# Token sums ahead of the output scale, a second token buffer and a later widening of z on GpSimd and VectorE

## The chip, the cores and the metric

The kernel runs on one core of a Trainium2 chip. The metric is the device time of one execution in microseconds, and the median of the runs counts. A core has TensorE (matrix products), VectorE, ScalarE and GpSimd, each with its own in-order queue, and SyncE (SP), whose queue issues most transfers here. TensorE writes to PSUM, the other engines read it from there; GpSimd works on SBUF alone.

## What is computed

```python
def reference(q, k, v, w_in, w_out, w_in2, w_out2, g_ln):     # cut to what matters
    # windowed attention: 4 batches, 8 heads, 576 positions, head size 64 (plain and dilated masks)
    x = attention(q, k, v)                     # 2304 tokens x 512
    h = x @ w_in                               # 512 x 2048
    x = (h - np.tanh(h)) @ w_out               # 2048 x 512
    h = x @ w_in2                              # 512 x 1024: the second layer
    e = np.exp(h - h.max(-1, keepdims=True))
    solu = h * e / (e.sum(-1, keepdims=True) + 1e-09)
    mu = solu.mean(-1, keepdims=True)
    var = ((solu - mu) ** 2).mean(-1, keepdims=True)
    return ((solu - mu) / np.sqrt(var + 1e-06) * g_ln) @ w_out2    # 1024 x 512
```

## The kernel before

Attention and the first layer take the first 507 us; the result y goes to a buffer in device memory, and the weights of the second layer are prepared beside the end of the first. The change lies in the second layer, which runs over nine pairs of token tiles. A pair is 256 tokens, an odd tile (2i + 1) and an even tile (2i) of 128 each. All products are done in a split form, a high and a low part of each operand with three matmuls in place of one.

`load_y` (L512 to L517) loads a pair of y into `yr`, one buffer. `split_y` (L519 to L541) forms combinations of the pair's four quarter blocks, for a scheme in which seven products take the place of eight. Its part 0 has four GpSimd operations on 128x256 elements (L530: three sums or differences into `ysm`, one back into `yr`), a VectorE copy of a high part (L537) and a GpSimd difference for the low part (L538). Parts 2 and 1 are a copy and a difference each: part 2 reads what the fourth sum wrote into `yr`, part 1 reads `ysm` (128x768).

`mm3(i)` (L639 to L681) runs the seven products of pair i on TensorE, six matmuls each, in the order p1, p6, p5, p7, p4, p2, p3 of the code's bank names (p3 is added into p5's bank). Four PSUM banks take turns, so the fifth product waits until VectorE's `u2` (L655) has read its bank, and the sixth until `u3` (L663) has read its own. The tree sums (`neg_add`, L636) add banks to h with the sign turned and take the minimum along the way. Then come `softmax_e` (exponential on ScalarE, L686), `softmax_u` (product with e, VectorE, L691), `softmax_z` (mean taken off, L697, L698) and `square` (ScalarE, L707, with a sum).

`fac` (L709) turns that sum on GpSimd into the variance and, with a power, into the factor `sc`. `split_z` (L741) splits the scaled z into two fp16 parts `ab` (ScalarE L745, VectorE L746), which a DMA transposes (SP, L749); `put_z` (L751) widens the high part on ScalarE (L756) and the low part on VectorE (L757). `rest` (L715) computes the output's scale `g` from the sums on GpSimd, six or seven operations on one column. `mm4` (L759) is the output product, 48 matmuls a pair, with a scaled copy out of PSUM (L769) and the store (L770). The tiles of pairs 0 and 8 go another way: `trz` (L728) transposes z on TensorE, without the factor in it.

The order on each engine is that in which the code issues. The loop at L784, for pair i: `square` and both `fac` of pair i + 1, parts 1 and 2 of `split_y(i + 2)` where i < 2, both `split_z`, both `rest`, a load where i < 2, the output products of pair i, and `mm3(i + 2)`. Inside that `mm3`, from pair 3 on, stand `split_y` part 0 of the next pair behind the second product, parts 1 and 2 and the load behind `u2`; `put_z` of the odd tile stands behind the third product, `put_z` of the even tile behind the fifth.

Of the kernel before, what the change touches and what calls it, by code (L numbers as in the profile page):

```python
# [7 lines left out]
F32 = mybir.dt.float32  # L8
F32R = mybir.dt.float32r
I32 = mybir.dt.int32  # L10
F16 = mybir.dt.float16
# [29 lines left out]
def tile_kernel(ctx: ExitStack, tc: tile.TileContext, qk, vw, cst, w_in, w_out, w_in2, w_out2, g_ln, out):  # L41
# [471 lines left out]

    def load_y(j):
        if j < NP:
            y_raw[j] = p2.tile([128, KD, YT], F32, tag="yr", name=f"yr{j}", bufs=1)
            nc.sync.dma_start(out=y_raw[j], in_=y_dr[:, :, j * YT:(j + 1) * YT])  # L517

    def split_y(j, parts=range(3)):  # L519

        if j >= NP:
            return
        r = y_raw[j]
        if 0 in parts:
            y = yt[j] = p2.tile([128, 2, 7, 2, TT], F32R, tag="yt", name=f"yt{j}")
            sm = y_sm[j] = p2.tile([128, 3, 2, TT], F32, tag="ysm", name=f"ysm{j}", bufs=1)
            a11, a21, a22 = r[:, 0:2, 0:TT], r[:, 0:2, TT:YT], r[:, 2:4, TT:YT]
            for o, a, b, op in ((sm[:, 0], a21, a22, ALU.add), (sm[:, 1], sm[:, 0], a11, ALU.subtract),
                                (sm[:, 2], a11, a21, ALU.subtract), (a21, r[:, 2:4, 0:TT], sm[:, 1], ALU.subtract)):
                nc.gpsimd.tensor_tensor(out=o, in0=a, in1=b, op=op)  # L530
        y, sm = yt[j], y_sm[j]
        yh = y[:, 0].rearrange("p s k t -> p (s k) t")
        yl = y[:, 1].rearrange("p s k t -> p (s k) t")
        for p, sl, v in ((0, slice(0, 4), r[:, :, 0:TT]), (2, slice(4, 8), r[:, :, TT:YT]),
                         (1, slice(8, 14), sm.rearrange("p s k t -> p (s k) t"))):
            if p in parts:
                nc.vector.tensor_copy(out=yh[:, sl], in_=v)  # L537
                nc.gpsimd.tensor_tensor(out=yl[:, sl], in0=v, in1=yh[:, sl].bitcast(F32), op=ALU.subtract)  # L538
        if 2 in parts:
            y_raw.pop(j)  # L540
            y_sm.pop(j)  # L541


    p2 = None
    nxt = []
    moe = None
    slot = 0
# [62 lines left out]
    sb = ctx.enter_context(tc.tile_pool(name="sb", bufs=1, space=PSUM, side="left", reuse_waits="tile"))  # L610
    zo = ctx.enter_context(tc.tile_pool(name="zo", bufs=2, space=PSUM, side="left", reuse_waits="tile"))
    p3 = ctx.enter_context(tc.tile_pool(name="p3", bufs=2, side="left", reuse_waits="tile"))
    st = {}

    def prod(ps, y, blk, w, first=True):
# [23 lines left out]
    def mm3(i, mid=()):  # L639

        y = yt.pop(i)
        for t in range(2):
            st[2 * i + t] = {}
        mid = dict(mid)
        b0, b1 = bank(sa, "b0", i, "p1"), bank(sa, "b1", i, "p6")
        prod(b0, y, 0, "b11")
        prod(b1, y, 5, "t2")
        if i > 2:
            split_y(i + 1, (0,))
        u2 = p3.tile([128, 512], F32, tag="u2", name=f"u2_{i}", bufs=1)  # L650
        u3 = p3.tile([128, 512], F32, tag="u3", name=f"u3_{i}", bufs=1)
        b2, b3 = bank(sb, "b2", i, "p5"), bank(sb, "b3", i, "p7")
        c = p3.tile([128, 512], F32, tag="c", name=f"c_{i}", bufs=1)
        nc.scalar.copy(out=c, in_=b0)
        nc.vector.tensor_tensor(out=u2, in0=b1, in1=c, op=ALU.add)  # L655
        if i > 2:
            split_y(i + 1, (1, 2))
            load_y(i + 2)
        prod(b2, y, 4, "t1")
        if 0 in mid:  # L660
            mid[0]()
        prod(b3, y, 6, "t3")
        nc.vector.tensor_tensor(out=u3, in0=b3, in1=u2, op=ALU.add)  # L663
        neg_add(i, 1, 1, b2, u3)
        b1 = bank(sa, "b1", i, "p4")
        prod(b1, y, 3, "t4")
        neg_add(i, 1, 0, b1, u3)
        if 1 in mid:
            mid[1]()
        softmax_e(2 * i + 1)  # L670
        b3 = bank(sb, "b3", i, "p2")
        prod(b3, y, 1, "b21")
        neg_add(i, 0, 0, b3, c)
        softmax_u(2 * i + 1)
        prod(b2, y, 2, "b22", first=False)
        neg_add(i, 0, 1, b2, u2)
        softmax_e(2 * i)
        softmax_z(2 * i + 1)
        square(2 * i + 1)
        softmax_u(2 * i)  # L680
        softmax_z(2 * i)  # L681
# [30 lines left out]
        nc.gpsimd.tensor_scalar(out=var, in0=var, scalar1=1.0 / FF2, scalar2=1e-36, op0=ALU.mult, op1=ALU.max)  # L712
        nc.gpsimd.tensor_tensor(out=sc, in0=var, in1=half, op=ALU.pow)

    def rest(i):  # L715

        d = st[i]
        ssum, sc, var, g = (d["sml"][:, c:c + 1] for c in (1, 4, 5, 6))
        nc.gpsimd.tensor_scalar(out=ssum, in0=ssum, scalar1=1e-9, scalar2=1e-3, op0=ALU.add, op1=ALU.mult)
        nc.gpsimd.tensor_tensor(out=ssum, in0=ssum, in1=ssum, op=ALU.mult)  # L720
        nc.gpsimd.tensor_tensor(out=ssum, in0=ssum, in1=var, op=ALU.add)
        nc.gpsimd.tensor_tensor(out=ssum, in0=ssum, in1=half, op=ALU.pow)
        nc.gpsimd.tensor_tensor(out=var, in0=var, in1=sc, op=ALU.mult)
        nc.gpsimd.tensor_tensor(out=g, in0=ssum, in1=var, op=ALU.mult)
        if i // 2 in (0, NP - 1):
            nc.gpsimd.tensor_tensor(out=g, in0=g, in1=sc, op=ALU.mult)

    def trz(i):  # L728

# [11 lines left out]
    def split_z(i):  # L741

        d = st[i]
        ab = p3.tile([128, 2, FF2], F16, tag="ab", name=f"ab{i}")
        nc.scalar.activation(out=ab[:, 0], in_=d["hn"], func=AF.Copy, scale=d["f"])  # L745
        nc.vector.scalar_tensor_tensor(out=ab[:, 1], in0=d["hn"], scalar=d["f"], in1=ab[:, 0], op0=ALU.mult,  # L746
                                       op1=ALU.subtract)
        t = d["zt"] = p3.tile([128, 2 * NF2, TT], F16, tag="zt", name=f"zt{i}")
        nc.sync.dma_start_transpose(out=t, in_=ab.rearrange("p a n -> p (a n)"))  # L749

    def put_z(i):  # L751

        d = st[i]
        z = d["z"] = p3.tile([128, 2, NF2, TT], F32R, tag="z", name=f"z{i}")
        t = d["zt"].rearrange("p (a j) t -> p a j t", a=2)
        nc.scalar.copy(out=z[:, 0], in_=t[:, 0])  # L756
        nc.vector.tensor_copy(out=z[:, 1], in_=t[:, 1])  # L757

    def mm4(i):  # L759
        d = st.pop(i)  # L760
# [9 lines left out]
        nc.sync.dma_start(out=out[i * TT:(i + 1) * TT, :], in_=o)  # L770

    mm3(0)
    fac(1)

    def first():
        trz(1)
        square(0)
        fac(0)
        split_y(2, (0,))
        rest(1)  # L780
        rest(0)

    mm3(1, {0: first, 1: lambda: trz(0)})
    for i in range(NP):  # L784
        o, e = 2 * i + 3, 2 * i + 2
        if i + 1 < NP:
            square(e)
            fac(o)
            fac(e)
        if i < 2:  # L790
            split_y(i + 2, (1, 2))
        if i + 2 < NP:
            split_z(o)
            split_z(e)
        if i + 1 < NP:
            rest(o)
            rest(e)
        if i < 2:
            load_y(i + 3)
        mm4(2 * i + 1)  # L800
        if i + 2 == NP:
            trz(o)
        mm4(2 * i)
        if i + 2 == NP:
            trz(e)
        if i + 2 < NP:
            mm3(i + 2, {0: lambda: (put_z(o), i == 0 and split_y(3, (0,))), 1: lambda: put_z(e)})
    p2.release()
    sa.release()

# [74 lines left out]
```

## Time and profile before

| | |
|---|---|
| median of three runs | 733.3 us (730.84 to 733.91) |
| the profiled execution | 733.56 us, its span 731.8 us |
| TensorE busy, share of the span | 692.7 us, 95% |
| VectorE | 479.0 us, 65% |
| ScalarE | 383.9 us, 52% |
| GpSimd | 205.8 us, 28% |
| mean granted clock of TensorE | 0.985 |
| start of the second layer | 507.6 us |

The profile is of one execution. Names such as `u` or `sml` are those of the program's tiles, L663 is a line of the kernel, and a bracket gives the idle time ahead of an instruction and the operation whose end ended it. Busy shares are means over stages with different limits, so the second layer is read by itself. The granted clock is the share of TensorE's full speed that was granted in a stretch.

### The profile page before, as it was taken

The page shows a single profiled execution, that of the slowest core. Times are in us where ns is not written, and L with a number is a line of the kernel's source. Part 1 is how long each engine was busy: PE and PEld are TensorE (multiplying, and loading weights), DVE is VectorE, ACT ScalarE, POOL GpSimd, SP SyncE. Part 2 cuts the span into 40 slices and gives each one's busy share as a digit, 9 for nine tenths or more (in the row PEclk, how much of TensorE's full clock was granted, in tenths as well). Part 3 has the DMA queues.
Part 4 walks back from the last instruction along what each step waited for, and adds up shares of the span by engine and source line. Part 5 has one row for each costly group of instructions (what it writes and reads, how often), then busy time and mean ns, then how long its engine had stood idle before and what let it go on. Part 6 is the DMA issues. An engine that isn't in the chain of part 4 may idle for free.

```text
span 731.8 us, 11282 instructions
## 1 busy us (share of the span) xinstructions
PE 692.7 (95%) x3994; PEld 638.2 (87%) x3994; DVE 479.0 (65%) x1157; ACT 383.9 (52%) x917; POOL 205.8 (28%) x276
## 2 busy tenths in 40 slices
PE   6898999999999999999999999999988598889897
PEld 5688899999999999999999999999866487677786
DVE  5987676476666667766666435996857457655650
ACT  5778775465555555555555333764454254345441
POOL 2212311011110111111100103750385655576521
PEclk9999999999999999999999999999999899999999
DMA  9976521232223221322230025452031542443121
GB/s 278 340 247 201 173 73 54 64 110 65 66 65 108 66 59 44 105 66 65 66 108 2 1 71 173 147 171 73 1 68 50 139 74 56 104 115 87 24 77 43
DMA packets 59431, 71.36 MB, mean 98 GB/s; under 512 B 32112, under 2 KB 45936, under 8 KB 59376
## 3 DMA queue, kind: packets, MB, share of 16 engines
q1 hardware_dynamic: 56208, 65.93, 30.9%
q10 hardware_dynamic: 3168, 4.72, 1.8%
q8 instruction: 31, 0.51, 0.3%
q14 instruction: 24, 0.20, 0.1%
HBM read 53.86 MB, written 9.44 MB: 87 GB/s over the span
## 4 chain that ended last, share of the span: by engine, by line
PE 73%; DVE 9%; POOL 8%; issue 4%; ACT 3%; DMA 2%; SPq 0%; ACTq 0%; POOLq 0%; DVEq 0%
PE y L381 28%; PE h L354 26%; PE po L766 6%; PE sp L620 5%; PE pv L281 2%; PE tp L260 2%; PE qkp L225 2%; PE qkp L205 2%; POOL ysm L530 1%; DMA yr<-y_dr 1%; POOL yt L538 1%; DVE z L757 1%; DVE hn L636 1%; DVE p L210 1%; ACT e L686 1%
## 5 line engine op out<-in xcount | busy, mean ns | idle before, releaser
L354 PE MATMUL h<-x,wi 128*128 128x384 f32 x1152 | 222.8, 342 | 1.1 <-DVE t L365 1.1
L381 PE MATMUL y<-gs,wo 128*128 128x384 f32 x1152 | 218.7, 338 | 0.0
L354 PEld LDWEIGHTS h<-x,wi 128*128 128x128 f32 x1152 | 200.9, 190 | 2.4 <-DVE t L365 1.3
L381 PEld LDWEIGHTS y<-gs,wo 128*128 128x128 f32 x1152 | 201.1, 189 | 1.8
L253 POOL TENSOR_TENSOR p<-p,rs 96x512 f32<-96x512 f32 x47 | 57.3, 1219 | 353.7 <-DVE rs L251 331.8
L365 DVE TENSOR_TENSOR t<-h,t 128x384 f32<-128x384 f32 x96 | 53.0, 552 | 79.0 <-ACT t L362 78.9
L766 PE MATMUL po<-w2o_o,z 128*128 128x512 f32 x432 | 100.7, 392 | 0.0
L371 DVE TENSOR_TENSOR gs<-t,gs 128x384 fp32r<-128x384 f32 x96 | 82.2, 856 | 23.4 <-ACT gs L368 23.3
L766 PEld LDWEIGHTS po<-w2o_o,z 128*128 128x128 f32 x432 | 81.1, 188 | 17.7
L362 ACT ACTIVATE t<-h 128x384 f32<-128x384 f32 x96 | 47.0, 489 | 93.7 <-PE h L354 90.4
L245 ACT ACTIVATE p<-p,nm 96x128 f32<-96x128 f32 x192 | 75.2, 394 | 21.2 <-DVE nm L210 20.8
L368 ACT CAST gs<-t 128x384 fp32r<-128x384 f32 x96 | 49.2, 512 | 49.2 <-DVE t L365 49.0
L620 PE MATMUL sp<-w2i_b,yt 128*128 128x512 f32 x162 | 46.6, 440 | 17.3 <-DVE u L663 17.3
L620 PEld LDWEIGHTS sp<-w2i_b,yt 128*128 128x128 f32 x162 | 34.3, 216 | 27.7 <-DVE u L663 20.1
L620 PE MATMUL sp<-w2i_t,yt 128*128 128x512 f32 x216 | 52.6, 398 | 4.8 <-DVE u L655 4.0
L686 ACT ACTIVATE e<-hn,sml 128x1024 f32<-128x1024 f32 x18 | 20.8, 1155 | 68.2 <-DVE sml L636 47.9
L620 PEld LDWEIGHTS sp<-w2i_t,yt 128*128 128x128 f32 x216 | 41.1, 192 | 14.2 <-DVE u L655 4.4
L245 ACT ACTIVATION_READ_ACCUMULATOR p<-p,nm 96x1 f32 x192 | 36.5, 190 | 0.0
L205 PE MATMUL qkp<-qkr 64*96 64x128 f32 x160 | 29.4, 339 | 7.2 <-DMA qkr<-in_qk_dram 5.4
L205 PEld LDWEIGHTS qkp<-qkr 64*96 64x96 f32 x160 | 24.1, 205 | 11.7 <-DMA qkr<-in_qk_dram 5.8
L292 DVE TENSOR_TENSOR x<-pv,x 128x384 fp32r<-128x384 f32 x24 | 16.4, 703 | 25.7 <-ACT x L290 25.2
L746 DVE SCALAR_TENSOR_TENSOR ab<-hn,sml,ab 128x1024 f16<-128x1024 f32 x14 | 22.2, 1630 | 15.9 <-ACT ab L745 15.9
(89 smaller groups left out, 858.0 us busy)
## 6 DMA issues: line engine op xcount, KB each, us to landing
qkr<-in_qk_dram SPq DMA_DIRECT2D x28, 448.0 KB, 3.4
raw_wi<-in_w_in_dram SPq DMA_DIRECT2D x16, 511.8 KB, 7.0
raw_wo<-in_w_out_dram SPq DMA_DIRECT2D x16, 511.8 KB, 7.4
v<-in_vw_dram SPq DMA_DIRECT2D x48, 128.0 KB, 3.3
y_dr<-ys ACTq DMA_DIRECT2D x6, 768.0 KB, 3.9
yr<-y_dr SPq DMA_DIRECT2D x9, 512.0 KB, 4.9
out_dram<-o SPq DMA_DIRECT2D x18, 256.0 KB, 2.6
qkr<-in_qk_dram SPq DMA_DIRECT2D x20, 224.0 KB, 5.2
```

The lines of the kernel that those rows point to most:

```text
L205: nc.tensor.matmul(ps[:, b], d["r"][:64, b * NQ:(b + 1) * NQ], d["r"][:64, QC + b * NK:QC + (b + 1) * NK], start=True, stop=True)
L245: nc.scalar.activation(out=d["p"][:, b], in_=d["p"][:, b], func=AF.Exp, scale=-1.0, bias=d["nm"][:, b:b + 1], accum_out=d["sm"][:, b:b + 1])
L253: eng.tensor_tensor(out=d["p"], in0=d["p"], in1=d["rs"].unsqueeze(2).to_broadcast([NQ, 4, NK]), op=ALU.mult)
L354: nc.tensor.matmul(ps, w[:, a, k * 128:(k + 1) * 128], xt[g, k][:, b], start=(n == 0), stop=(n == 3 * KD - 1))
L362: nc.scalar.activation(out=t, in_=ps, func=AF.Tanh)
L365: nc.vector.tensor_tensor(out=t, in0=ps, in1=t, op=ALU.subtract)
L368: nc.scalar.copy(out=gs[:, 0], in_=t)
L371: nc.vector.tensor_tensor(out=gs[:, 1], in0=t, in1=gs[:, 0].bitcast(F32), op=ALU.subtract)
L381: nc.tensor.matmul(yb[g][m], wo[c][:, a, m * 128:(m + 1) * 128], gs[:, b], start=(c == 0 and i == 0), stop=(c == NF - 1 and i == 2))
L620: nc.tensor.matmul(ps, y[:, a, blk, kk], w2i[w, kk][:, b], start=first and q == 0, stop=q == 5, skip_group_check=not first)
L686: nc.scalar.activation(out=d["e"], in_=d["hn"], func=AF.Exp, bias=d["sml"][:, 0:1], scale=-1.0, accum_out=d["sml"][:, 1:2])
L766: nc.tensor.matmul(po, z[:, a, j], w2o[j][:, b], start=(q == 0), stop=(q == 3 * NF2 - 1))
```

## The change

In `first` and in the loop, part 0 of `split_y` is issued ahead of `rest`, and the `rest` of the even tile moves to the end of the next `mm3`, as the third of its middle steps. The yr of odd pairs from 3 on has a buffer of its own in pool `p3`, pair 3 is loaded when that pool is made, and the other loads come one pair earlier. `put_z` is cut in two: the high part of the odd tile behind the third product, its low part behind the fifth together with the high part of the even tile, and that one's low part behind the seventh. `fac` is left out for pairs 0 and 8, whose `rest` computes the scale in one power. `ab` uses the buffer of `e`.

```diff
--- before.py
+++ after.py
@@ -513,7 +513,8 @@
 
     def load_y(j):
         if j < NP:
-            y_raw[j] = p2.tile([128, KD, YT], F32, tag="yr", name=f"yr{j}", bufs=1)
+            pool = p3 if j > 2 and j % 2 else p2
+            y_raw[j] = pool.tile([128, KD, YT], F32, tag="yr", name=f"yr{j}", bufs=1)
             nc.sync.dma_start(out=y_raw[j], in_=y_dr[:, :, j * YT:(j + 1) * YT])
 
     def split_y(j, parts=range(3)):
@@ -541,7 +542,7 @@
             y_sm.pop(j)
 
 
-    p2 = None
+    p2 = p3 = None
     nxt = []
     moe = None
     slot = 0
@@ -610,6 +611,7 @@
     sb = ctx.enter_context(tc.tile_pool(name="sb", bufs=1, space=PSUM, side="left", reuse_waits="tile"))
     zo = ctx.enter_context(tc.tile_pool(name="zo", bufs=2, space=PSUM, side="left", reuse_waits="tile"))
     p3 = ctx.enter_context(tc.tile_pool(name="p3", bufs=2, side="left", reuse_waits="tile"))
+    load_y(3)
     st = {}
 
     def prod(ps, y, blk, w, first=True):
@@ -645,17 +647,15 @@
         b0, b1 = bank(sa, "b0", i, "p1"), bank(sa, "b1", i, "p6")
         prod(b0, y, 0, "b11")
         prod(b1, y, 5, "t2")
-        if i > 2:
-            split_y(i + 1, (0,))
         u2 = p3.tile([128, 512], F32, tag="u2", name=f"u2_{i}", bufs=1)
         u3 = p3.tile([128, 512], F32, tag="u3", name=f"u3_{i}", bufs=1)
         b2, b3 = bank(sb, "b2", i, "p5"), bank(sb, "b3", i, "p7")
         c = p3.tile([128, 512], F32, tag="c", name=f"c_{i}", bufs=1)
         nc.scalar.copy(out=c, in_=b0)
         nc.vector.tensor_tensor(out=u2, in0=b1, in1=c, op=ALU.add)
-        if i > 2:
+        if i > 1:
             split_y(i + 1, (1, 2))
-            load_y(i + 2)
+            load_y(i + 3)
         prod(b2, y, 4, "t1")
         if 0 in mid:
             mid[0]()
@@ -674,6 +674,8 @@
         softmax_u(2 * i + 1)
         prod(b2, y, 2, "b22", first=False)
         neg_add(i, 0, 1, b2, u2)
+        if 2 in mid:
+            mid[2]()
         softmax_e(2 * i)
         softmax_z(2 * i + 1)
         square(2 * i + 1)
@@ -712,18 +714,21 @@
         nc.gpsimd.tensor_scalar(out=var, in0=var, scalar1=1.0 / FF2, scalar2=1e-36, op0=ALU.mult, op1=ALU.max)
         nc.gpsimd.tensor_tensor(out=sc, in0=var, in1=half, op=ALU.pow)
 
-    def rest(i):
+    def rest(i, trz=False):
 
         d = st[i]
         ssum, sc, var, g = (d["sml"][:, c:c + 1] for c in (1, 4, 5, 6))
+        if trz:
+            nc.gpsimd.tensor_scalar(out=var, in0=var, scalar1=1.0 / FF2, scalar2=None, op0=ALU.mult)
         nc.gpsimd.tensor_scalar(out=ssum, in0=ssum, scalar1=1e-9, scalar2=1e-3, op0=ALU.add, op1=ALU.mult)
         nc.gpsimd.tensor_tensor(out=ssum, in0=ssum, in1=ssum, op=ALU.mult)
         nc.gpsimd.tensor_tensor(out=ssum, in0=ssum, in1=var, op=ALU.add)
-        nc.gpsimd.tensor_tensor(out=ssum, in0=ssum, in1=half, op=ALU.pow)
-        nc.gpsimd.tensor_tensor(out=var, in0=var, in1=sc, op=ALU.mult)
-        nc.gpsimd.tensor_tensor(out=g, in0=ssum, in1=var, op=ALU.mult)
-        if i // 2 in (0, NP - 1):
-            nc.gpsimd.tensor_tensor(out=g, in0=g, in1=sc, op=ALU.mult)
+        if trz:
+            nc.gpsimd.tensor_tensor(out=g, in0=ssum, in1=half, op=ALU.pow)
+        else:
+            nc.gpsimd.tensor_tensor(out=ssum, in0=ssum, in1=half, op=ALU.pow)
+            nc.gpsimd.tensor_tensor(out=var, in0=var, in1=sc, op=ALU.mult)
+            nc.gpsimd.tensor_tensor(out=g, in0=ssum, in1=var, op=ALU.mult)
 
     def trz(i):
 
@@ -741,20 +746,23 @@
     def split_z(i):
 
         d = st[i]
-        ab = p3.tile([128, 2, FF2], F16, tag="ab", name=f"ab{i}")
+        ab = d["e"].bitcast(F16).rearrange("p (a n) -> p a n", a=2)
         nc.scalar.activation(out=ab[:, 0], in_=d["hn"], func=AF.Copy, scale=d["f"])
         nc.vector.scalar_tensor_tensor(out=ab[:, 1], in0=d["hn"], scalar=d["f"], in1=ab[:, 0], op0=ALU.mult,
                                        op1=ALU.subtract)
         t = d["zt"] = p3.tile([128, 2 * NF2, TT], F16, tag="zt", name=f"zt{i}")
         nc.sync.dma_start_transpose(out=t, in_=ab.rearrange("p a n -> p (a n)"))
 
-    def put_z(i):
+    def put_z(i, part):
 
         d = st[i]
-        z = d["z"] = p3.tile([128, 2, NF2, TT], F32R, tag="z", name=f"z{i}")
+        if part == 0:
+            d["z"] = p3.tile([128, 2, NF2, TT], F32R, tag="z", name=f"z{i}")
         t = d["zt"].rearrange("p (a j) t -> p a j t", a=2)
-        nc.scalar.copy(out=z[:, 0], in_=t[:, 0])
-        nc.vector.tensor_copy(out=z[:, 1], in_=t[:, 1])
+        if part == 0:
+            nc.scalar.copy(out=d["z"][:, 0], in_=t[:, 0])
+        else:
+            nc.vector.tensor_copy(out=d["z"][:, 1], in_=t[:, 1])
 
     def mm4(i):
         d = st.pop(i)
@@ -770,41 +778,43 @@
         nc.sync.dma_start(out=out[i * TT:(i + 1) * TT, :], in_=o)
 
     mm3(0)
-    fac(1)
 
     def first():
         trz(1)
         square(0)
-        fac(0)
         split_y(2, (0,))
-        rest(1)
-        rest(0)
 
     mm3(1, {0: first, 1: lambda: trz(0)})
     for i in range(NP):
         o, e = 2 * i + 3, 2 * i + 2
+        last = i + 2 == NP
         if i + 1 < NP:
             square(e)
-            fac(o)
-            fac(e)
-        if i < 2:
-            split_y(i + 2, (1, 2))
-        if i + 2 < NP:
-            split_z(o)
-            split_z(e)
-        if i + 1 < NP:
-            rest(o)
-            rest(e)
-        if i < 2:
-            load_y(i + 3)
+            if last:
+                rest(o, True)
+                rest(e, True)
+            else:
+                fac(o)
+                if i == 0:
+                    split_y(2, (1, 2))
+                fac(e)
+                if i == 0:
+                    rest(1, True)
+                    rest(0, True)
+                split_z(o)
+                split_z(e)
+                split_y(i + 3, (0,))
+                rest(o)
+                if i == 0:
+                    load_y(4)
         mm4(2 * i + 1)
-        if i + 2 == NP:
+        if last:
             trz(o)
         mm4(2 * i)
-        if i + 2 == NP:
+        if last:
             trz(e)
         if i + 2 < NP:
-            mm3(i + 2, {0: lambda: (put_z(o), i == 0 and split_y(3, (0,))), 1: lambda: put_z(e)})
+            mm3(i + 2, {0: lambda: put_z(o, 0), 1: lambda: (put_z(o, 1), put_z(e, 0)), 2: lambda: (put_z(e, 1), rest(e))})
     p2.release()
     sa.release()
```

## Rows read from the trace of the kernel before

**Rows 1.** Waits of TensorE from 490 us: us in total, times, longest.
```profile
PE sp L620 <- DVE u L663: 17.3, 6, 4.2
```

**Rows 2.** Second layer, stretches between starts of output products: us, busy, clock, DMA.
```profile
556.22:587.81 31.59, 23.96 (x91) 18.70 (x90) 18.88 (x28) 10.77 (x15) 17.79 (x25) 0.89 0.35 84
...
635.68:658.44 22.76, 20.83 (x91) 16.82 (x90) 14.51 (x25) 10.59 (x15) 14.59 (x23) 1.00 0.39 93
...
683.54:704.07 20.53, 20.53 (x91) 16.90 (x90) 11.44 (x23) 10.66 (x15) 6.65 (x16) 1.00 0.34 77
```

**Rows 3.** The same view, two stretches behind a wait.
```profile
631.30:635.70 4.40, 4.39 (x13) 3.49 (x14) 3.48 (x8) 1.24 (x2) 1.03 (x1) 0.63 0.41 123
655.60:658.40 2.80, 2.80 (x12) 2.35 (x13) 2.65 (x7) 1.13 (x2) 1.02 (x1) 1.00 0.63 187
```

**Rows 4.** Timeline of TensorE: start, us, engine, line, operation, tiles, [idle before].
```profile
539.54 1.52 PE L620 MATMUL sp<-w2i_b,yt 128*128 128x512 f32 x6
...
631.31 4.53 PE L620 MATMUL sp<-w2i_b,yt 128*128 128x512 f32 x12 [2.85 <-DVE u L663]
...
655.59 3.01 PE L620 MATMUL sp<-w2i_b,yt 128*128 128x512 f32 x12 [1.93 <-DVE u L663]
...
701.35 2.88 PE L620 MATMUL sp<-w2i_b,yt 128*128 128x512 f32 x12
```

**Rows 5.** Timeline of GpSimd, one pair and the next `fac`.
```profile
642.02 0.55 POOL L713 TENSOR_TENSOR sml<-sml,half 128x1 f32<-128x1 f32 x1
...
648.18 0.74 POOL L530 TENSOR_TENSOR ysm<-yr 128x256 f32<-128x256 f32 x1
...
651.22 1.29 POOL L538 TENSOR_TENSOR yt<-yr,yt 128x512 fp32r<-128x512 f32 x1
...
654.35 2.27 POOL L538 TENSOR_TENSOR yt<-ysm,yt 128x768 fp32r<-128x768 f32 x1
...
665.68 0.56 POOL L713 TENSOR_TENSOR sml<-sml,half 128x1 f32<-128x1 f32 x1
```

**Rows 6.** Timeline of VectorE, the same pair.
```profile
642.71 2.48 DVE L746 SCALAR_TENSOR_TENSOR ab<-hn,sml,ab 128x1024 f16<-128x1024 f32 x2 [2.32 <-ACT ab L745]
645.10 0.42 DVE L537 CAST yt<-yr 128x512 fp32r<-128x512 f32 x1
...
651.29 1.50 DVE L537 CAST yt<-yr 128x512 fp32r<-128x512 f32 x1 [0.91 <-POOL yr L530]
...
653.18 1.76 DVE L757 CAST z<-zt 128x1024 fp32r<-128x1024 f16 x1
654.86 0.68 DVE L663 TENSOR_TENSOR u<-sp,u 128x512 f32<-128x512 f32 x1
...
658.55 1.23 DVE L691 SCALAR_TENSOR_TENSOR hn<-hn,e 128x1024 f32<-128x1024 f32 x1 [0.16 <-ACT e L686]
...
659.70 0.75 DVE L636 CUSTOM_DVE_ANT_0 hn<-sp,u,sml 128x512 f32<-128x512 f32 x1
```

**Rows 7.** Timeline of all engines, a collision in the first pass.
```profile
538.47 4.84 DVE L746 SCALAR_TENSOR_TENSOR ab<-hn,sml,ab 128x1024 f16<-128x1024 f32 x2 [2.83 <-ACT ab L745]
...
539.43 2.81 POOL L538 TENSOR_TENSOR yt<-ysm,yt 128x768 fp32r<-128x768 f32 x1
```

**Rows 8.** Timeline of all engines, fp16 split, transposes and widening of one pair.
```profile
642.61 1.15 ACT L745 ACTIVATE ab<-hn,sml 128x1024 f16<-128x1024 f32 x1
...
644.02 4.57 SPq L749 DMA_TRANSPOSE zt<-ab  x2
...
650.81 1.05 ACT L756 CAST z<-zt 128x1024 fp32r<-128x1024 f16 x1 [1.02 <-DMA zt<-ab]
```

**Rows 9.** Timeline of GpSimd, the first sum of pair 3.
```profile
550.74 0.97 POOL L530 TENSOR_TENSOR ysm<-yr 128x256 f32<-128x256 f32 x1 [3.45 <-DMA yr<-y_dr]
```

**Rows 10.** Timeline of VectorE, the product with e of the first pass.
```profile
528.44 2.14 DVE L691 SCALAR_TENSOR_TENSOR hn<-hn,e 128x1024 f32<-128x1024 f32 x1
```

**Rows 11.** Timeline of ScalarE, end of the first pass's square of tile 3.
```profile
533.45 0.19 ACT L707 ACTIVATION_READ_ACCUMULATOR e<-hn 128x1 f32 x1
```

## Prediction

> **What bounds the kernel now.** I read the busy shares first: TensorE is busy 95% of the span, so a change off TensorE can only return the rest. The list of waits then says where that rest is: from 490 us on TensorE waits 17.3 us in six stalls for VectorE's u of L663 [rows 1]; a few more go to another u and to GpSimd. Third, the table of stretches cuts the second layer at the starts of its output products [rows 2]: the last pair of tokens but one costs 20.53 us and TensorE never idles in it; the pairs before it cost 22.76 to 31.59 us. So the price of a pair without a wait is 20.53 us, and the distance to it is what can be won. It is more than the waits, since the clock falls behind the long ones: after an idle of 2.85 us the stretch has a granted clock of 0.63, a mean between the levels 1.2 and 2.4 GHz, and twelve matmuls take 4.4 us; after 1.93 us it has 1.00 and they take 2.8 [rows 3, 4].
>
> Fourth, the timelines of GpSimd and VectorE in one such pair say what u waits for. `fac` ends at 642.57 (642.02 + 0.55); then come two `rest`, and only at 648.18 the token sums, whose last feeds the difference that starts at 651.22 [rows 5]. VectorE's copy of the high part waits for the sums and then stands behind that difference (1.50 us, where the copy at 645.10 takes 0.42); behind it, in order, come the copy of the sums, the widening of z (1.76) and at last u (L663) at 654.86 [rows 6]. From there to the next `fac`: the last tree sum of the pair starts at 659.70, the next `fac` ends at 666.24 (665.68 + 0.56), 6.54 us later [rows 5, 6]. This closed loop over VectorE, ScalarE and GpSimd, not TensorE, sets a pair's time.
>
> **The collisions.** When VectorE's fp16 split (`ab`) meets a GpSimd difference, each op waits for the whole of the other: two `ab` took 4.84 us, where they take 2.48 at 642.71, and the 128x768 difference beside them 2.81 [rows 6, 7]. With `ab` at 1.15 that difference alone is about 1.64 (2.81 less one `ab`). VectorE's u, with one operand in PSUM, is not held up: 0.68 us at 654.86 while a difference ran [rows 5, 6]. The Trainium skill, SBUF — State Buffer, "Who interferes with whom", says that VectorE's two-port and two-input instructions and GpSimd take the shared port pair as an exclusive lock and the loser "fully blocks"; these rows agree, and were the port shared without blocking, the sum would be that of the first rival.
>
> **The change, part by part.**
> 1. *Sums ahead of `rest`, in pairs 3 to 7.* Count from the end of `fac` (T). Four sums at 0.76 (651.22 - 648.18 over four) [rows 5], the two `ab` at 1.15 and one copy at 0.42 [rows 6], which now fall into the same time and collide, and the difference at 1.29: 3.04 + 2.30 + 0.42 + 1.29 = 7.05. Before, the two `ab` were hidden beside the two `rest`; that cover is gone, 2.3 us. Call the end of this difference Q.
> 2. *What GpSimd does behind Q.* `rest` of the odd tile: (648.18 - 642.57) / 2 = 2.8 with its share of collisions; I take 2.7 with the two copies beside it. The second difference 1.29, a widening of z that cuts in 0.65, the third difference 1.64. GpSimd is through at Q + 6.3. `rest` of the even tile follows behind the third difference, where only the next `fac`, five us later, stands behind it: nothing.
> 3. *What VectorE does behind Q.* Copy of the high part, copy of the sums: Q + 1.1. Then u (L663), two tree sums, and at Q + 3.3 the widening of the odd tile's z, which now stands behind the fifth product. It meets the second difference and runs from Q + 4.0 to 4.65. The product with e (L691) comes at 5.5, meets the third difference and runs from Q + 6.3 to 7.45. The last tree sum starts at Q + 7.45; 6.54 later, and 0.15 for the even tile's widening that is put in (0.65, mostly beside the exponential that is awaited there), `fac` ends.
>    The loop is 7.05 + 7.45 + 6.69 = 21.2 us. That is still over 20.53: TensorE will wait for u some 0.6 us in each pair, under the 1.93 after which the clock stayed [rows 3].
>    Does the late widening hold the output product? u ends at Q + 1.8, and the output product starts two products (704.07 - 701.35 = 2.72) behind [rows 2, 4]: Q + 4.55; it reads the low part at its third product, Q + 5.0, and has it at 4.65. Margin 0.35.
> 4. *The transposes* start 0.7 later (behind the first `ab`); issue to arrival of the second is 6.8 [rows 8], so T + 8.9, and ScalarE's widening ends at T + 9.9, ahead of the exponential at Q + 3.3 = T + 10.4: nothing. `ab` in the buffer of e: the same transposes release it before that exponential. Nothing, by the same cover.
> 5. *Own buffer for odd pairs.* Pair 3 is loaded as the stage begins. Before, its sums waited 3.45 us for it [rows 9]. The load may wait for weight buffers of the stage before, and holds only SP, whose next work are the transposes of the first pass. Pair 4's load stands behind those transposes and its sums are some 15 us off; later loads are a whole pair ahead.
> 6. *First pass.* TensorE does the same to 539.54, the first product of pair 2 [rows 4]. GpSimd's sums of pair 2 lose 14 small instructions ahead of them and run early, beside VectorE's last weight work: bounds 0 and four collisions of 0.76, 3 us; the second layer's first product stands in TensorE's queue behind output products of the first layer that were ready before, and I take 0. The first difference then runs before the product with e at 528.44, which shrinks from 2.14 to the 1.23 it has alone [rows 6, 10]: 0.91 earlier, so the square ends at 532.73, not 533.64 [rows 11], and `fac` at 533.95 (1.2 behind it). Pair 2's second and third difference: 534.35 to 537.3. `ab` 1.12, then `fac` of the even tile 0.8: 539.2. ScalarE's `ab`, 1.15 [rows 8]: 540.4; VectorE's to 541.55. Two `rest` of pair 0, five instructions each, 1.65 each and 1.1 of collision: 543.65. Sums of pair 3, 3.04: 546.7; difference 1.29: Q = 548.0. u follows at Q + 1.1 to 1.8, where the fifth product ended near 547.05: TensorE waits 2.7 us there and up to 0.7 for the first u. The output product starts at 552.5, or 554.1 at the low clock, instead of 556.22; the loop behind it hides that difference.
> 7. *Fewer instructions* (`rest` of pairs 0 and 8 without `fac`): 12 small ones, at the tail hidden by output products.
>
> **Sum.** Five loops from Q = 548.0: 548.0 + 5 x 21.2 = 654.0; the output product of pair 6 starts 4.55 behind, 658.5, where it now starts at 683.54. From there nothing changes: 731.8 - 683.54 = 48.26. Span 706.8; the profiled execution took 733.56, 1.76 over its span, and the median is 733.3, 0.3 less, which I leave out. Forecast 708.5 us, 25 us faster.
>
> **Rivals.**
> - *TensorE becomes the bound.* If the collisions cost little (ops slip past each other, `rest` is short), pairs fall to 20.53. From 552.5: five times 20.53 is 655.2, span 703.4, 705.2 us; with the first pass free of waits too (539.54 and seven products at 1.36 = 549.1), 701.8. For: the loop is only 0.7 over. Against: the ops that collide add up to 14.6 of these 20.5 us (sums 3.0, differences 4.2, `ab` 2.3, copies 1.4, z 1.3, products with e 2.4). Chance 0.25.
> - *The loop loses once more.* The widening of z arrives while the third difference runs instead of the second (it needs 0.65 us of lateness), and ends at Q + 5.65 or later; loop 22.1, output product held 0.3 each time: 5 x 0.9 more, 713 us. If two such losses come each pair, 23.0: 717.5. Against: GpSimd has to be through before L691 either way. Chance 0.13.
> - *Sums don't matter.* If copies or z, not sums, are what u waits for, the pairs keep their time: 733. Against: the copy's idle ends with the sums in each pair. Chance 0.03.
> - *Slower: the transposes come late.* They stand behind `ab`, which now collides, and ScalarE's in-order queue has the exponential behind their widening. From 2 us of further lateness (T + 11.9 against L691 at T + 13.3 with 1.35 of exponential ahead) each us enters the loop. To eat 25 us and 3.7 more over five pairs it takes 5.7 + 2 us of lateness per pair; the transposes needed 6.8 where they collided least. Time 737.5 at that point. Chance 0.03.
>
> **Chances and range.** Forecast 0.56, between 705.5 and 711.5 (0.6 us per loop and 1 us of the first pass in question). The range takes in the first two rivals without their extremes: 702.5 to 715. Half a percent, 3.7 us, is what can be told from no change. Faster 0.94, same 0.03, slower 0.03.
>
> **What will show it.** In the changed kernel's GpSimd timeline the sums stand right behind the second `fac`, interleaved with `ab`, and the two `ab` take about 4 us. Waits of TensorE for u (L663) fall from 17.3 to about 5 us, most of it in pair 2, and no stretch behind 560 us has a clock below 0.98. The stretches between output products are 21 to 21.5 us and no longer alternate. The product with e (L691) shows 2 us where the third difference runs. Wrong would be: stretches of 20.5 (the collisions are cheaper than I count), stalls of the output product for z (the widening is too late), or exponentials that wait for transposes.

## The result

The changed kernel takes 704.5 us (median of 4 runs, 703.45 to 706.61) against 732.63 us for the kernel before in the same comparison: a ratio of 0.9621, with a 95% interval of 0.9588 to 0.9654. The forecast was 708.5 us. The profiled execution took 706.61 us, its span is 704.8 us.

The waits of TensorE from 480 us on, which answer to [rows 1]:

```profile
PE sp L622 <- DVE u L663: 2.0, 1, 2.0
PE sp L622 <- DVE u L655: 0.6, 1, 0.6
```

The 17.3 us of waits for the u of L663 are 2.0 us, in one stall; the 0.6 are a wait for `u2`. The stretches between the starts of output products (columns as in [rows 2]: length, busy times of TensorE, its weight loads, VectorE, ScalarE and GpSimd, granted clock, transfers):

```profile
528.74:554.08 25.34, 22.67 (x92) 17.94 (x90) 16.77 (x27) 10.71 (x15) 19.22 (x30) 0.93 0.40 90
554.08:574.58 20.50, 20.50 (x91) 16.90 (x90) 14.29 (x26) 10.86 (x15) 18.07 (x27) 1.00 0.48 120
...
595.09:615.60 20.51, 20.51 (x92) 16.90 (x90) 14.45 (x26) 10.87 (x15) 15.32 (x24) 1.00 0.43 103
...
656.61:677.12 20.51, 20.51 (x92) 16.90 (x91) 11.91 (x23) 10.86 (x15) 7.98 (x19) 1.00 0.34 78
```

Only the first is over 20.5 us. The pairs that cost 31.59 to 22.76 us in [rows 2] now cost what the last stretch there cost, 20.53, in which TensorE never idled: TensorE is the bound from 554 us on, and the output product of pair 6 starts at 656.61 instead of 683.54. That is all of the difference of the spans: 26.9 of 27.0 us.

One pair on GpSimd and on VectorE, which answers to [rows 5, 6]:

```profile
622.54 0.55 POOL L715 TENSOR_TENSOR sml<-sml,half 128x1 f32<-128x1 f32 x1
623.06 0.74 POOL L531 TENSOR_TENSOR ysm<-yr 128x256 f32<-128x256 f32 x1
623.88 1.61 POOL L531 TENSOR_TENSOR ysm<-ysm,yr 128x256 f32<-128x256 f32 x1
625.45 1.72 POOL L531 TENSOR_TENSOR ysm<-yr 128x256 f32<-128x256 f32 x1
627.24 0.80 POOL L531 TENSOR_TENSOR yr<-yr,ysm 128x256 f32<-128x256 f32 x1
628.01 1.29 POOL L539 TENSOR_TENSOR yt<-yr,yt 128x512 fp32r<-128x512 f32 x1
629.38 0.19 POOL L723 TENSOR_SCALAR sml<-sml 128x1 f32<-128x1 f32 x1
...
631.38 1.30 POOL L539 TENSOR_TENSOR yt<-yr,yt 128x512 fp32r<-128x512 f32 x1
632.63 1.85 POOL L539 TENSOR_TENSOR yt<-ysm,yt 128x768 fp32r<-128x768 f32 x1
```

```profile
623.23 3.34 DVE L751 SCALAR_TENSOR_TENSOR e<-hn,sml,e 128x1024 f16<-128x1024 f32 x2 [2.32 <-ACT e L750]
626.49 0.96 DVE L538 CAST yt<-yr 128x512 fp32r<-128x512 f32 x1
...
632.22 0.69 DVE L663 TENSOR_TENSOR u<-sp,u 128x512 f32<-128x512 f32 x1 [1.16 <-PE sp L622]
...
634.47 0.69 DVE L765 CAST z<-zt 128x1024 fp32r<-128x1024 f16 x1
...
635.92 1.23 DVE L693 SCALAR_TENSOR_TENSOR hn<-hn,e 128x1024 f32<-128x1024 f32 x1 [0.16 <-ACT e L688]
```

The sums stand right behind `fac` (ends 623.09) and alternate with the two `ab`: 3.34 us for these where they took 2.48. The first difference ends at 629.30, 6.2 us behind `fac`. u waits for nothing but its product on TensorE, and VectorE idles 1.16 us ahead of it. The widening of z (0.69) and the product with e (1.23) meet no difference any more: the third ends at 634.48, just as the widening comes.

The first pass, on TensorE:

```profile
545.98 1.66 PE L622 MATMUL sp<-w2i_t,yt 128*128 128x512 f32 x6 [0.65 <-DVE u L655]
549.66 4.57 PE L622 MATMUL sp<-w2i_b,yt 128*128 128x512 f32 x12 [2.03 <-DVE u L663]
```

### The profile page after: what moved, and what is told of

The parts are those of the page before. It is cut to its first block, busy times and chain, and to the rows that moved or that the text cites. A ratio compares the mean times of both kernels' runs of the same rounds, so it can differ in the third digit from the quotient of the medians.

```text
span 704.8 us, 11283 instructions
## 1 busy us (share of the span) xinstructions
PE 685.0 (97%) x3994; PEld 634.7 (90%) x3994; DVE 473.3 (67%) x1157; ACT 384.5 (55%) x917; POOL 206.0 (29%) x260
## 4 chain that ended last, share of the span: by engine, by line
PE 90%; DVE 4%; POOL 2%; DMA 1%; issue 1%; ACT 1%; SPq 0%; POOLq 0%; ACTq 0%
PE y L381 29%; PE h L354 29%; PE po L774 12%; PE sp L622 11%; PE pv L281 2%; PE qkp L205 2%; PE tp L260 2%; PE qkp L225 2%; DVE p L210 1%; DMA qkr<-in_qk_dram 1%; DVE wy_wi L129 1%; DMA raw_wi<-in_w_in_dram 1%; DVE wi L104 1%; PE zp L741 0%; POOL yt L539 0%
## 5 line engine op out<-in xcount | busy, mean ns | idle before, releaser
L622 PE MATMUL sp<-w2i_t,yt 128*128 128x512 f32 x216 | 51.1, 390 | 0.6 <-DVE u L655 0.6
L622 PE MATMUL sp<-w2i_b,yt 128*128 128x512 f32 x162 | 41.3, 402 | 2.0 <-DVE u L663 2.0
L622 PEld LDWEIGHTS sp<-w2i_b,yt 128*128 128x128 f32 x162 | 31.4, 195 | 9.0 <-DVE u L663 2.5
L539 POOL TENSOR_TENSOR yt<-yr,yt 128x512 fp32r<-128x512 f32 x18 | 24.9, 1384 | 37.8 <-DVE yt L538 32.5
L751 DVE SCALAR_TENSOR_TENSOR e<-hn,sml,e 128x1024 f16<-128x1024 f32 x14 | 23.0, 1674 | 17.4 <-ACT e L750 17.4
```

What stands on the lines that cost most here:

```text
L622: nc.tensor.matmul(ps, y[:, a, blk, kk], w2i[w, kk][:, b], start=first and q == 0, stop=q == 5, skip_group_check=not first)
```

## The experiments

The first theory after the result: TensorE sets a pair's time, the loop over GpSimd, VectorE and ScalarE lies below it, and the order of the sums has done it. The rivals: the loop is only just below, so that the later widening and the later `rest` are needed too; or the second buffer carries the gain.

**The order alone.** The kernel before, with the sums of pairs 5 to 8 ahead of `rest`:

```diff
-        if i > 2:
+        if i == 3:
             split_y(i + 1, (0,))          # in mm3
...
+        if i > 1:
+            split_y(i + 3, (0,))          # in the loop, ahead of rest(o), rest(e)
```

> The kernel before with one edit: from pair 5 on, the four token sums are issued ahead of both rest steps; buffers, loads and the widening of z stay. Four pairs are touched, the output products of pairs 2 to 6, which take 95.7 us before. Theory S (the order of the sums carries the gain of a pair by itself): these four fall to 20.5 us each, 82 us, and the time to 719 to 720 us. Theory R (the later widening of z and the even tile's rest at the end of the products are needed too): counted anew with the lengths read from the changed kernel (6.2 us from fac to the end of the first difference, both rest 4 us, differences 3.1 us, product with e 1.2, 6.5 us to the next fac) the loop is 21.0 us, TensorE waits about 0.5 us for u in each pair, and the time is 721 to 723 us.

Measured 719.55 us, ratio 0.9824 (0.9797 to 0.9852). That is theory S, for the four pairs that this edit touches. The output products of pairs 2 to 6 start at 586.90, 607.64, 628.14, 648.65 and 669.16: 82.3 us for the four pairs, and TensorE waits in none of them. Theory R counted on the widening ahead of u and on a collision of the product with e. Both are there, but they cost no time:

```profile
643.53 0.69 DVE L757 CAST z<-zt 128x1024 fp32r<-128x1024 f16 x1
644.77 0.69 DVE L663 TENSOR_TENSOR u<-sp,u 128x512 f32<-128x512 f32 x1 [0.56 <-PE sp L620]
...
648.72 2.26 DVE L691 SCALAR_TENSOR_TENSOR hn<-hn,e 128x1024 f32<-128x1024 f32 x1
```

In this timeline of VectorE the widening stands ahead of u and the product with e waits a microsecond for the third difference (2.26 us), yet VectorE still idles 0.56 us for TensorE.

**The change without its order.** Both `rest` back ahead of the sums:

```diff
+                rest(o)
+                rest(e)
                 split_y(i + 3, (0,))
-                rest(o)
...
-2: lambda: (put_z(e, 1), rest(e))
+2: lambda: put_z(e, 1)
```

> The changed kernel with both rest steps put back ahead of the sums; the buffers, the loads and the later widening of z stay. Theory S: the whole gain of the pairs is lost, 22.8 us or more a pair, 715 to 722 us. Theory R: the widening that no longer stands ahead of u gives back part of it; the loop is rest 5.6, sums 3.1, difference 1.3, then 5.0 to the product with e and 6.7 to the next fac, 21.7 us; TensorE hides 1.7 us of the first pairs' lateness and the time is 708 to 711 us.

Measured 717.69 us, ratio 0.9803 (0.9776 to 0.983): 13 us of the gain are gone. Its TensorE timeline:

```profile
553.92 5.49 PE L622 MATMUL sp<-w2i_b,yt 128*128 128x512 f32 x12 [5.67 <-DVE u L663]
...
621.98 3.02 PE L622 MATMUL sp<-w2i_b,yt 128*128 128x512 f32 x12 [1.53 <-DVE u L663]
...
644.32 3.01 PE L622 MATMUL sp<-w2i_b,yt 128*128 128x512 f32 x12 [1.53 <-DVE u L663]
```

A pair is 22.34 us (644.32 - 621.98), between the two theories (21.7 and 22.8 or more); over four pairs that is 7.3 us more than in the changed kernel. Most of the rest is a wait of 5.67 us in the first pass, which neither had priced.

**The widening alone undone.**

```diff
-{0: lambda: put_z(o, 0), 1: lambda: (put_z(o, 1), put_z(e, 0)), 2: lambda: (put_z(e, 1), rest(e))}
+{0: lambda: (put_z(o, 0), put_z(o, 1)), 1: lambda: (put_z(e, 0), put_z(e, 1)), 2: lambda: rest(e)}
```

> The changed kernel with the widening of z as before: low part of the odd tile behind the third product, so ahead of u, and the even tile's behind the fifth. If the later widening carries part of the gain: the 0.7 us, or 1.7 us where it meets a GpSimd difference, stand ahead of u in each pair, TensorE waits up to 1 us a pair, 707 to 710 us. If TensorE's bound leaves it room (VectorE idles 1.16 us ahead of u in the changed kernel): 704 to 705 us, no wait of TensorE in pairs 3 to 7.

Measured 706.41 us, ratio 0.9643 (0.9614 to 0.9672), an interval that overlaps with the changed kernel's; the median lies between the two expectations. TensorE waits nowhere behind pair 2. What the later widening buys there is room, 0.6 us of it: VectorE's idle ahead of u is 0.56 us here where it was 1.16. In pair 2, where there is no room, it shows: TensorE waits 2.63 us for u in place of 2.03.

```profile
612.87 0.69 DVE L663 TENSOR_TENSOR u<-sp,u 128x512 f32<-128x512 f32 x1 [0.56 <-PE sp L622]
```

**The even tile's `rest` alone undone**, beside that of the odd tile, behind the sums:

```diff
                 rest(o)
+                rest(e)
...
-2: lambda: (put_z(e, 1), rest(e))
+2: lambda: put_z(e, 1)
```

> The changed kernel with the rest step of the even tile put back beside that of the odd tile, so 1.8 us of GpSimd work ahead of the second and third difference, behind the sums. Theory A (GpSimd's chain is tight): the product with e waits for the third difference 1.6 us longer, loop 21.9 us, 704.5 + 5 x 1.4 - 1.7 = 710 us. Theory B (room): 704 to 706 us, the product with e shows 2 us or more where the third difference runs, and TensorE waits nowhere behind pair 2.

Measured 703.35 us, ratio 0.9604 (0.9579 to 0.963): nothing lost. The product with e waits (1.62 to 1.88 us in place of 1.23), as theory B said, though by less than its 2 us, and behind pair 2 TensorE does not.

**One buffer.** The change with one `yr` buffer, the loads where they were, and the sums of pairs 3 and 4 where they must then stand (parts 1 and 2 of pair 3 stand in the loop again, too; this part of the edit is left out below):

```diff
-            pool = p3 if j > 2 and j % 2 else p2
+            pool = p2
...
-            load_y(i + 3)                 # in mm3
+            load_y(i + 2)
```

> The changed kernel with one buffer for the tokens of all pairs and with their loads where the kernel before has them; the sums of pairs 3 and 4 stand where they stood. If the second buffer serves the first pass alone: TensorE waits about 4 us for u in pair 2 as before, the output product of pair 1 starts near 556 to 557 us instead of 554.1, pair 3 costs 1 to 3 us more for pair 4's sums behind their load, and the time is 707 to 711 us; pairs 4 to 7 stay at 20.5 us. If the buffer serves every pair: 712 us or more, with sums waiting for their load in each pair.

Measured 717.55 us, ratio 0.9794 (0.9767 to 0.9822), which neither expectation explains: the buffer serves the first two passes alone, as the first said, but with the places of the sums that go with it it is worth 13 us there, not 3 to 6; the time is in the second's range, but no load is waited for behind pair 4. GpSimd's timeline has two waits for loads:

```profile
547.80 0.96 POOL L531 TENSOR_TENSOR ysm<-yr 128x256 f32<-128x256 f32 x1 [3.82 <-DMA yr<-y_dr]
...
573.43 0.96 POOL L531 TENSOR_TENSOR ysm<-yr 128x256 f32<-128x256 f32 x1 [6.79 <-DMA yr<-y_dr]
```

The second, ahead of pair 4's sums, made TensorE wait 6.18 and 1.94 us in pair 3, whose output product starts 32.9 us behind the one before. The stretch before that takes 24.57 us (527.12 to 551.69), where two executions of the changed kernel have 25.34 and 23.78, so the 13 us lie in pair 3. Behind it the pairs take 20.97 us once and then 20.5.

**The buffer alone.** The kernel before with the second buffer and the earlier loads (and `ab` in the buffer of e, as in the change, to make room; its own share was not taken apart):

```diff
+            pool = p3 if j > 2 and j % 2 else p2
+    load_y(3)                             # where p3 is made
-            load_y(i + 2)
+            load_y(i + 3)                 # in mm3
-            load_y(i + 3)
+            load_y(i + 4)                 # in the loop, i < 2
```

> The kernel before with the second token buffer and the loads one pair earlier (and the fp16 split in the buffer of e, which makes the room for it); the order of sums and rest stays. If buffer and order add up: the waits for the load go (3.45 us ahead of pair 3's sums, 3.80 us ahead of pair 4's, with the low clock behind them), pairs 4 to 8 keep 22.8 to 25.2 us, 724 to 727 us; the order then gives the other 20 us or so. If the buffer gives nothing without the order, since rest stands ahead of the sums anyway: 731 to 733 us.

Measured 722.76 us, ratio 0.9872 (0.9849 to 0.9894): 9.3 us by the buffer, a little more than expected for the case that buffer and order add up (724 to 727 us). Together with the 13.5 us of the order in four pairs that is 23 of the change's 28 us. Between the output products of pairs 1 and 2 this kernel takes 28.87 us (550.11 to 578.98) and the changed kernel 20.50: 8.4 us that the buffer leaves and the rest of the change takes away. Against it stands a loss. The first pass takes 21.56 us here (528.55 to 550.11) and 25.34 in the changed kernel, where the `rest` of pair 0 stands behind the second `fac`, ahead of the sums of pair 3; the experiment on the first pass, below, takes that up. The pairs behind still wait for u, behind `rest`:

```profile
573.91 5.23 PE L622 MATMUL sp<-w2i_b,yt 128*128 128x512 f32 x12 [5.86 <-DVE u L665]
...
622.93 3.01 PE L622 MATMUL sp<-w2i_b,yt 128*128 128x512 f32 x12 [1.57 <-DVE u L665]
```

**How far below TensorE the loop lies.** The third sum is issued two or four times more in pairs 4 to 8 (the output is the same):

```diff
-(sm[:, 2], a11, a21, ALU.subtract),
+*[(sm[:, 2], a11, a21, ALU.subtract)] * (3 if j > 3 else 1),      # 5 for four more
```

> The changed kernel with the third token sum issued two more times (same operands, same result) in pairs 4 to 8: 1.5 us more of GpSimd work in the loop, between fac and the first difference. It measures how far the loop lies under TensorE's 20.5 us. Theory A (GpSimd's chain is all but tight: its third difference ends where VectorE's widening of z asks for the port, 0.2 us of room): the loop is 21.8 us, TensorE hides some 1.7 us of the lateness once, and the time is 704.5 + 5 x 1.3 - 1.7 = 709.5 us, with waits for u in the last pairs. Theory B (VectorE idles 1.16 us ahead of u, and 0.47 us more lie between u and its product: 1.6 us of room): 704.5 to 705 us, no new wait. By the forecast's loop of 21.2 us, now 22.7: 712 us or more.

> The same with four more sums a pair, 3.0 us. Theory A: loop 23.3 us, 704.5 + 5 x 2.8 - 1.7 = 717 us. Theory B: loop 1.4 us over TensorE's, which shows in each pair from the first on as a wait of 1.4 us for u: 704.5 + 5 x 1.4 = 711.5 us. No difference to one two times shorter would mean that the sums are not in the loop at all.

Measured 707.69 us, ratio 0.9658 (0.9631 to 0.9684), with two more, and 715.48 us, ratio 0.9761 (0.9737 to 0.9784), with four. Now the loop is the bound, and its length can be read from the spacing of u on VectorE, first with two more sums, then with four:

```profile
569.96 0.68 DVE L663 TENSOR_TENSOR u<-sp,u 128x512 f32<-128x512 f32 x1
590.96 0.68 DVE L663 TENSOR_TENSOR u<-sp,u 128x512 f32<-128x512 f32 x1
611.96 0.68 DVE L663 TENSOR_TENSOR u<-sp,u 128x512 f32<-128x512 f32 x1
```

```profile
571.44 0.68 DVE L663 TENSOR_TENSOR u<-sp,u 128x512 f32<-128x512 f32 x1
594.04 0.68 DVE L663 TENSOR_TENSOR u<-sp,u 128x512 f32<-128x512 f32 x1
616.65 0.68 DVE L663 TENSOR_TENSOR u<-sp,u 128x512 f32<-128x512 f32 x1
```

21.00 and 22.60 us: 0.80 us a sum. Without them the loop is 21.00 - 1.60 = 19.4 us, 1.1 below TensorE's 20.5. Theory A (0.2 of room) and the forecast's 21.2 are wrong, and no theory had both times; theory B's idle of 1.16 us is the room, without the 0.47 it added, which can be spent once and not in each pair.

**The first pass.** The two `rest` of pair 0 are issued in the products of pair 1:

```diff
-                if i == 0:
-                    rest(1, True)
-                    rest(0, True)
...
-    mm3(1, {0: first, 1: lambda: trz(0)})
+    mm3(1, {0: first, 1: lambda: (trz(0), rest(1, True), rest(0, True))})
```

> The changed kernel with the two rest steps of pair 0 issued in the products of pair 1, where GpSimd idles (it has nothing from 526 to 533 us), in place of between the second fac and the sums of pair 3 in the first pass. If these 4.3 us of GpSimd work are what makes TensorE wait 0.65 and 2.0 us in pair 2 (and run its two last products at the low clock in the profiled execution): the waits go, the output product of pair 1 starts at 549.5 instead of 554.1, and the time is 700.5 to 702 us. If the first pass only moves the lateness into pair 3 (the loop has no room): TensorE waits there, 703 to 705 us.

Measured 701.14 us, ratio 0.957 (0.9545 to 0.9595). TensorE has no wait left in the second layer; from one output product to the next it takes 20.5 us in the first pass too. (The output product of pair 1 starts at 548.00, not at 549.5, as that of pair 0 starts 1.25 us earlier in this execution.)

```profile
527.49 11.15 PE L774 MATMUL po<-w2o_o,z 128*128 128x512 f32 x48
548.00 11.15 PE L774 MATMUL po<-w2o_o,z 128*128 128x512 f32 x48
```

**Only the parts that count.** The same with the widening back where the kernel before has it and the even tile's `rest` beside the odd tile's, behind the sums; and the changed kernel again beside it.

> The kernel of the first-pass experiment (rest of pair 0 in the products of pair 1) with two parts of the change undone at once: the widening of z where the kernel before has it, and the even tile's rest beside the odd tile's. Each of these alone cost nothing that shows. If there is room for both (1.1 us in the loop): 701 to 702 us as without the undoing. If together they fill it: the loop goes to 21 us as in the kernel with the order alone, TensorE waits some 0.3 us in the later pairs, 702.5 to 704 us.

> The changed kernel once more, beside the two others on the same chip, for a comparison with the first-pass version: 703.5 to 705.5 us, with a wait of 2.0 us for u in pair 2.

Measured on the same chip: 700.94 us, ratio 0.9579 (0.9559 to 0.9598), and 704.91 us, ratio 0.9631 (0.9604 to 0.9659). The intervals do not overlap, so this version, with the order, the buffer and the earlier `rest` of pair 0, beats the changed kernel; the two parts undone are worth nothing that the times show, alone or together. (The single power of pairs 0 and 8 and `ab` in the buffer of e are in it too; no run takes them out.) One wait is left, in the first pass, where the widening stands ahead of u:

```profile
546.90 3.06 PE L622 MATMUL sp<-w2i_b,yt 128*128 128x512 f32 x12 [0.34 <-DVE u L663]
```

## Why the prediction was right or wrong

The bound and the cause were read rightly: taking `rest` from ahead of the sums, alone, brings the touched pairs to 20.5 us, and putting it back makes them 22.34 us and loses 13 us. The forecast of 25 us was 3 to 4 us short. The case that had the chance of 0.56, 705.5 to 711.5 us, did not come: 704.5 lies below it. What came was the first rival, TensorE as the bound, with 705.2 us forecast and a chance of 0.25, and the range holds the time because it takes that rival in. The signs say the same: stretches of 20.5 us, which the prediction had named as the sign of being wrong, 2.0 us of waits for u and not about 5, two `ab` in 3.34 us and not about 4, and no 2 us for the product with e.

Some of the closeness is luck. In the profiled execution the output product of pair 6 starts at 656.61, forecast 658.5: five loops were each 0.7 us shorter than forecast, 3.5 us, and 1.6 us of low clock in the first pass, which the forecast took to be hidden, came on top.

*First pass (step 6): right, term by term.* The first difference of pair 3 was to end at 548.0 and ended at 548.27; u was to start at 549.1 and started at 548.93; waits of up to 0.7 and of 2.7 us were 0.65 and 2.03; the output product of pair 1 was to start at 552.5, or 554.1 at the low clock, and started at 554.08 with a granted clock of 0.93 in its stretch. That the waits come from the two `rest` of pair 0 is shown by the version without them. One reason given there is wrong, as is the same point in the description of the change: in the kernel before, the 14 instructions of the two `rest` stood behind the sums of pair 2, not ahead. Ahead of them stood the two `fac`, which wait for the squares (27.03 us idle in its trace), and without these the sums run at 494.4.

*The loop (steps 1 to 3): right in its members and their order, 1.8 us too long.* The run with two more sums has the loop as the bound and shows each leg. GpSimd, then VectorE:

```profile
602.89 0.55 POOL L715 TENSOR_TENSOR sml<-sml,half 128x1 f32<-128x1 f32 x1
603.41 0.74 POOL L531 TENSOR_TENSOR ysm<-yr 128x256 f32<-128x256 f32 x1
604.23 1.60 POOL L531 TENSOR_TENSOR ysm<-ysm,yr 128x256 f32<-128x256 f32 x1
...
609.99 1.30 POOL L539 TENSOR_TENSOR yt<-yr,yt 128x512 fp32r<-128x512 f32 x1
...
613.36 1.29 POOL L539 TENSOR_TENSOR yt<-yr,yt 128x512 fp32r<-128x512 f32 x1
614.61 2.31 POOL L539 TENSOR_TENSOR yt<-ysm,yt 128x768 fp32r<-128x768 f32 x1
...
623.89 0.55 POOL L715 TENSOR_TENSOR sml<-sml,half 128x1 f32<-128x1 f32 x1
```

```profile
614.19 1.02 DVE L765 CAST z<-zt 128x1024 fp32r<-128x1024 f16 x1
...
615.74 2.27 DVE L693 SCALAR_TENSOR_TENSOR hn<-hn,e 128x1024 f32<-128x1024 f32 x1
...
617.93 0.74 DVE L638 CUSTOM_DVE_ANT_0 hn<-sp,u,sml 128x512 f32<-128x512 f32 x1
```

- `fac` ends at 603.44, the first difference at 611.29: 7.85, less 1.60 for the added sums 6.25. Forecast 7.05. I charged each `ab` with its whole length and the copy with 0.42. The 1.15 us for it is ScalarE's row [rows 8]; VectorE's two take 2.48 [rows 6], 1.24 each, so the full charge would have been larger still. The two sums that met an `ab` took 1.61 and 1.72 us in the changed kernel instead of 0.74, so an `ab` costs 0.87 to 0.98, and the copy next to nothing.
- From there to the last tree sum, at 617.93: 6.64. Forecast 7.45. `rest` ran from 611.37 to 613.41, 2.0 us instead of 2.7, which is most of it. The two collisions that I had placed, the widening with the second difference (1.02) and the product with e with the third (2.27), are both there. The third difference, without a collision, takes 1.85 us in the changed kernel (632.63) and not the 1.64 that I had got by taking a whole `ab` off 2.81.
- From the last tree sum to the end of the next `fac`, 624.44: 6.51. Forecast 6.69; the even tile's widening costs nothing.

So 6.25 + 6.64 + 6.51 = 19.4 in place of 21.2. As the loop is below 20.5 us, what depended on its being above fell too: in the changed kernel itself TensorE comes first; from pair 3 on the widening and the product with e arrive behind the differences and collide with nothing, and the 2 us forecast for the latter are 1.23. "The loop behind it hides" the low clock of the first pass fell as well. In the repeat the same two products ran at full clock, and the stretch was 23.8 us (526.89 to 550.67) instead of 25.3. That execution took 703.31 us, the first 706.61; 1.6 of the 3.3 us are this stretch, and 1.85 lie ahead of it.

*Steps that were costed at nothing.* The transposes: ScalarE's widening at 631.71 ends well ahead of the exponential at 634.65, which waits for VectorE. The early sums of pair 2 (494.4 to 498.9) made VectorE's weight work about 2 us later, and the second layer still began behind a TensorE that never waited. Both held. The later widening and the later `rest` were part of the plan of steps 2 and 3, not terms of gain, and the runs agree that they gain nothing that the times show.

*The buffer (step 5)* I had left without a price of its own. It is worth 9 us alone, of which 6.1 in the first pass (27.67 us before, 21.56 with it), and 13 with the rest of the change, nearly all in pair 3, where pair 4's sums would wait 6.8 us for a load.

*The rivals.* More losses, sums that don't matter, and late transposes did not come. (By its own terms the last would be at 737.2 us, 708.5 + 28.7, and not at 737.5; step 7 leaves out 16 small instructions, four a tile, and not 12. Neither bears on the result.)

## What to carry to other kernels

When an engine's waits repeat in each step of a loop, add up the closed loop through the other engines and compare it with the bound engine's own time for a step: what counts is which is longer, and work may be put into the shorter one for free up to the difference. Where the two sums lie as close as here (21.2 against 20.5 us, when the first was 1.8 off), give both outcomes like chances, and measure the difference by adding a known dummy operation until the time moves. Charge a collision of GpSimd and VectorE by how much a blocked operation grew in the trace, not by the duration of the one that blocked it.

## What was not expected of the hardware

*A collision costs less than the operation that causes it.* An `ab` of 1.24 us held a sum up by 0.87 and 0.98 us (1.61 and 1.72 where it takes 0.74), and the 0.42 us copy hardly showed. The kernel before has it already, in its GpSimd timeline: an operation on one column takes 1.11 us beside an `ab` and 0.19 beside nothing, 0.92 more.

```profile
642.93 1.11 POOL L720 TENSOR_TENSOR sml<-sml 128x1 f32<-128x1 f32 x1
...
645.90 0.19 POOL L723 TENSOR_TENSOR sml<-sml 128x1 f32<-128x1 f32 x1
```

The Trainium skill, SBUF — State Buffer, "Who interferes with whom", says of VectorE's 2-port modes that whoever issues first has the port pair it shares with GpSimd for the whole instruction, and that the other fully blocks; instructions with two SBUF inputs, as `ab` is one, contend too by that section. That is right in kind here, but with the profile's durations in the sum it gave 0.8 us too much for one stretch.

*The clock behind a wait of about 2 us is not settled by the wait.* With four more sums, TensorE waited 1.80 us twice for the same u, and the granted clock of the stretches behind differs:

```profile
594.80:597.60 2.80, 2.80 (x12) 2.33 (x13) 2.65 (x6) 1.15 (x2) 2.72 (x5) 1.00 0.00 0
617.40:621.80 4.40, 4.40 (x12) 3.48 (x13) 4.12 (x8) 1.24 (x2) 4.24 (x6) 0.61 0.21 62
```

The twelve matmuls take 2.8 us in one and 4.4 in the other, 1.6 us apart (0.61 is a mean between the levels 1.2 and 2.4 GHz). The wait of 2.03 us in the first pass was followed by either, in two executions of the same program: by 4.57 us for the twelve matmuls above, and in the repeat by 3.00. With the buffer alone a wait of 1.78 us already had the slow ones behind it.

```profile
547.84 3.00 PE L622 MATMUL sp<-w2i_b,yt 128*128 128x512 f32 x12 [2.03 <-DVE u L663]
```

```profile
598.73 4.61 PE L622 MATMUL sp<-w2i_b,yt 128*128 128x512 f32 x12 [1.78 <-DVE u L665]
```

What decides it is not shown here; I had taken 1.93 us to be safe from one row [rows 3, 4].
